# Order of wide and narrow matmuls in two accumulations of an attention, expert and MLP kernel

## The chip, the cores and the metric

The kernel runs on one core of a Trainium2 chip. The metric is the device time of one execution in microseconds. Before the change it is 5529.54 us, the median of 3 runs (5529.25 to 5530.24).

## The reference

Three layers follow one another, in float32:

```python
# attention: u, v (8, 3072, 256), z (8, 3072, 64)
scores = (1.0 / S) * np.matmul(z, z.transpose(0, 2, 1))
attn = np.maximum(scores, 0.0) ** 2
x = (u * np.matmul(attn, v)).reshape(B * S, D)          # 24576 rows of 256
# experts: 8 of them, each row goes to one
xn, en = x / (norm(x) + 1e-6), emb / (norm(emb) + 1e-6)
logits = xn @ en.T / tau
expert_idx = argmax(logits); gate_w = softmax(logits)[expert_idx]
out[mask_e] = gate_w * (np.maximum(x[mask_e] @ w1[e], 0) @ w2[e])   # w1 256x1024, w2 1024x256
# MLP: w_in 256x2048, w_out 2048x256
h = x @ w_in
g = np.where(h > 0, h, np.exp(np.minimum(h, 0)) - 1)
return g @ w_out
```

## The kernel before, in words

TensorE works on float32r operands. To keep float32's accuracy, an operand is split into `hi`, its float32r part, and `lo`, the rest, and a product is made of three: hi x hi, hi x lo and lo x hi. In the two accumulations that the change touches the right-hand tile holds both parts side by side: columns 0 to 255 are the hi part of v (or of w_out), columns 256 to 511 its lo part. One matmul with `hi` as weights over all 512 columns gives hi x hi and hi x lo at once, and one with `lo` as weights over the first 256 columns gives lo x hi, added onto the first half.

The work is a list of steps, which a loop at L1328 emits in order. In step n the loop emits the first matmuls of step n (`"h"`), the splitting of step n-1 on VectorE (`"d1"` to `"d4"`), any matmuls due here such as transposes (`pre`), the accumulation of step n-2 (`"acc"`, since LAG is 2), the elementwise part of step n on ScalarE (`"g"`), and then the loads, stores and small operations that were planned for the step. Each engine runs its instructions in this order.

Attention has 48 chunks of 512 query rows and 12 steps for each, 576 in all. `att_h` (L358) makes four 512-column matmuls for 256 keys, ScalarE takes relu and square, ScalarE or VectorE makes `hi`, VectorE `lo`, and `att_acc` (L401) adds `hi`, `lo` times v onto four accumulators, one for each 128 query rows `q`, for the two key tiles `j`. The last step of a chunk empties accumulators 0 and 1 as soon as they are done, then 2 and 3.

After that come units of the expert stage and of the MLP, mixed: 41 A units (512 rows of one expert, four steps with 512-column matmuls), 21 B units (256 rows, two steps with 256-column matmuls), 41 M units (the MLP of an A unit) and 7 D units (the MLP of rows that B units made). M and D have eight steps each. In one, `m_h` (L926) makes twelve 512-column matmuls, ScalarE and VectorE work out the activation and split it, and `m_acc` (L1019) is the same accumulation as in attention, with w_out in place of v. The very last D unit has functions of its own (`l_h`, `l_acc`). `xt_ops` (L835) transposes the rows of an A or D unit, eight small matmuls that stand ahead of the accumulation two steps before that unit starts.

`hi` and `lo` take slots of one ring of 48; a slot is free when its last reader is done. Every matmul is emitted by the helper at L102, so that all have this line in the profile, and each has a weight load of its own (its first operand).

Of the kernel before, what the change touches and what calls it, by code (L numbers as in the profile page):

```python
# [27 lines left out]
def attn_moe_mlp(ctx, tc, zT, u, v, emb, tau, wp, w_in, w_out, out):  # L28
# [99 lines left out]
    loadD, loadA = defaultdict(float), defaultdict(float)  # L128

    def fill(L, n0, n1, d, a, off):  # L130
        """steps for L operations, in order, that even out the load of their engine"""
        load, c, o = (loadD, d, off) if d else (loadA, a, 0)
        n1 = max(n1, n0 + 1)
        if not c:
            return [n0 + i * (n1 - n0) // L for i in range(L)]
        lo, hi = 0.0, 100.0
        for _ in range(40):
            mid = (lo + hi) / 2
            fits = sum(int(max(0.0, mid - load[w + o]) / c + 0.5) for w in range(n0, n1))
            lo, hi = (lo, mid) if fits >= L else (mid, hi)  # L140
        out = []
        for w in range(n0, n1):
            out += [w] * int(max(0.0, hi - load[w + o]) / c + 0.5)
        out = out[:L]
        for w in out:
            loadD[w + off] += d
            loadA[w] += a
        return out
# [4 lines left out]
            tasks[w][s].append(fn)  # L153

    def pairs(fns, n0, n1, d=0.0, a=0.0):
        """the second half of each pair comes a step after the first"""
        s = stream()
        for i, w in enumerate(fill(len(fns) // 2, n0, n1, d, a, 1)):
            tasks[w][s].append(fns[2 * i])
            tasks[w + 1][-s].append(fns[2 * i + 1])  # L160
# [68 lines left out]
                         zt.bitcast(F32).rearrange("p (t d) -> p t d", t=4))  # L229

    def inv_norm_ops(n2, inv, w):
        """inv = 1/(sqrt(n2)+1e-6) as a list of single operations"""
        h = {}

        def a0():
            h["z"] = t_sm()[:, :w]
            h["t"] = t_sm()[:, :w]
            ts(h["t"].bitcast(I32), n2.bitcast(I32), 1, ALU.logical_shift_right)
        ops = [a0, lambda: ts(h["z"].bitcast(I32), h["t"].bitcast(I32), -1, ALU.mult, 0x5F3759DF, ALU.add)]
        for c in (1.0, 0.25, 0.0625):  # L240
            ops += [lambda c=c: stt(h["t"], h["z"], c, n2, ALU.mult, ALU.mult),
                    lambda: tt(h["t"], h["t"], h["z"], ALU.mult),
                    lambda: stt(h["z"], h["t"], 3.0, h["z"], ALU.subtract, ALU.mult)]
        ops += [lambda: stt(h["t"], h["z"], -0.125, n2, ALU.mult, ALU.mult),
                lambda: ts(h["t"], h["t"], 1e-6, ALU.add),
                lambda: vec.reciprocal(inv, h["t"])]
        return ops
# [27 lines left out]
            return fn  # L275
        return [ld], [n2(e) for e in range(E)] + [late] + [sc(e) for e in range(E)]

# [1 line left out]
    P, Q, V, X, XE, UT, AC, HL, PS = {}, {}, {}, {}, {}, {}, {}, {}, {}  # L279
    n2t, dott = {}, {}  # L280

    def z_ops(b, c2, parts=1):
        """P = [hi; lo], Q = [lo; hi] of two chunks"""
        h = {}

        def ld(w=slice(0, 2)):
            if "z" not in h:
                h["z"] = slot("zz")
            src = zT[b, :, c2 * 1024 + w.start * 512:c2 * 1024 + w.stop * 512]
            for q in range(2):  # L290
                sp.dma_start(flat(h["z"][:, w])[q * 64:(q + 1) * 64], src)

        def o1(w):
            def fn():
                if (b, c2) not in P:
                    P[b, c2] = rslot("zp")
                cp(P[b, c2][:, w], h["z"][:, w])
            return fn

        def o2(w):  # L300
            def fn():
                p = P[b, c2][64:128, w]
                tt(p, h["z"][64:128, w], f(p), ALU.subtract)
            return fn
        def direct(w):
            def fn():
                for d, nm in ((P, "zp"), (Q, "zq")):
                    if (b, c2) not in d:
                        d[b, c2] = rslot(nm)
                z_, p, q = h["z"][:, w], P[b, c2][:, w], Q[b, c2][:, w]  # L310
                cp(p[0:64], z_[0:64])
                cp(q[64:128], z_[64:128])
                tt(q[0:64], z_[0:64], f(p[0:64]), ALU.subtract)
                tt(p[64:128], z_[64:128], f(q[64:128]), ALU.subtract)
            return fn
        ws = [slice(i * 2 // parts, (i + 1) * 2 // parts) for i in range(parts)]
        if c2 == 0 == b:
            return ld, [direct(w) for w in ws]
        return ld, [o for w in ws for o in (o1(w), o2(w))]
# [81 lines left out]
    def att_acc(C, m):  # L401
        b, c = divmod(C, NC)
        if m == 0:
            AC[C] = [t_acc(), t_acc()]
        hi, lo = HL.pop((C, m))
        last = m == CS - 1
        vt = V[b, m]
        for q in range(4):
            a = AC[C][q // 2][:, q % 2]
            sl = slice(q * 128, q * 128 + 128)  # L410
            for j in range(2):
                st = last and j == 1
                mm(a, hi[:, j, sl], vt[:, j], m == 0 and j == 0, st)
                mm(a[:, :256], lo[:, j, sl], vt[:, j, :256], False, st)
            if last and q % 2 == 1:
                if q == 1:
                    X[C] = slot("x", F32, (4, 256))
                    XE[C] = slot("xe", F32, (4, 256))
                ap = AC[C][q // 2]
                cp(XE[C][:, q - 1:q + 1], ap[:, :, 256:])  # L420
                cp(X[C][:, q - 1:q + 1], ap[:, :, :256])
# [157 lines left out]
            return fn  # L579
        return seg1, rank, seg2, [scat(t) for t in range(T)], [scale(t) for t in range(T)]  # L580

# [1 line left out]
    arena = {}  # L583

    def keep(name, shape, dt=F32):
# [75 lines left out]
        tt(o[:, :, 1:], c[:, :, :E - 1], c[:, :, 1:], ALU.subtract)  # L661

    def tile_plan_ops(J, Fn, cumF, tag, taken):
        """first rows of J full tiles and their experts' weight rows"""
        h = {}

        def k3(n):
            h[n] = keep(n + tag, [128, J, E])
            return h[n]

        def k2(n):
            h[n] = keep(n + tag, [128, J])
            return h[n]

        ops = [
            lambda: tt(k3("cmp"), b2(K["jt"][:, :J], J, E), bj(K[cumF], J), ALU.is_ge),
            lambda: red(k2("e"), h["cmp"], ALU.add),
            lambda: ts(k2("w"), h["e"], 128.0, ALU.mult, K["pcol"], ALU.add),
            lambda: vec.tensor_copy(keep("wi" + tag, [128, J], I32), h["w"]),
            lambda: ts(keep("reg" + tag, [128, E]), K[Fn], -512.0, ALU.mult, float(N), ALU.add),  # L680
            lambda: tt(k3("t"), h["cmp"], bj(K["reg" + tag], J), ALU.mult),
            lambda: red(k2("s"), h["t"], ALU.add),
            lambda: stt(h["s"], K["jt"][:, :J], 512.0, h["s"], ALU.mult, ALU.add),
            lambda: onehot(k3("oh"), h["cmp"]),
        ]
        if taken is None:
            ops += [lambda: red(keep("taken" + tag, [128, E]), h["oh"].rearrange("p j e -> p e j"), ALU.add)]
        else:
            ops += [
                lambda: tt(h["oh"], h["oh"], bj(K[taken], J), ALU.mult),  # L690
                lambda: red(k2("ta"), h["oh"], ALU.add),
                lambda: stt(h["s"], h["ta"], 512.0, h["s"], ALU.mult, ALU.add)]

        def ix():
            h["ix"] = keep("ixf" + tag, [128, J, 4])
            tt(h["ix"], b2(h["s"], J, 4), tpj(J, 4), ALU.add)
        return ops + [ix, lambda: vec.tensor_copy(keep("ix" + tag, [128, J, 4], I32), h["ix"])]
# [68 lines left out]

        return ops + [arena.clear]

# [1 line left out]
    W1, W2, XT, IDS, WST, WI, WO, X2 = {}, {}, {}, {}, {}, {}, {}, {}  # L770

    def gather(dst, src, idx, bound):
# [60 lines left out]
        return [gi(t) for t in range(nt)] + [gx(t) for t in range(nt)], h  # L833

    def xt_ops(key, h, dst, nt):  # L835
        """transposes of the rows and their two parts"""
        def tr():
            p = t_ps()
            h["p"] = p if nt == 4 else p[:, 0].rearrange("p (a b) -> p a b", a=2)
# [179 lines left out]
    def m_acc(key, i):  # L1019
        if i == 0:  # L1020
            AC[key] = [t_acc(), t_acc()]
        hi, lo = HL.pop((key, i))
        w = WO[i]
        last = i == NF2 // 2 - 1
        for q in range(4):
            a = AC[key][q // 2][:, q % 2]
            sl = slice(q * 128, q * 128 + 128)
            for j in range(2):
                st = last and j == 1
                mm(a, hi[:, j, sl], w[:, j], i == 0 and j == 0, st)  # L1030
                mm(a[:, :256], lo[:, j, sl], w[:, j, :256], False, st)
            if last and q % 2 == 1:
                if q == 1:
                    PS[key] = slot("o", F32, (4, 256)), slot("o2", F32, (4, 256))
                o, t = PS[key]
# [25 lines left out]
        return ld, xt_ops(key, h, X2, 4)  # L1061

    def conv_ops(src, store):
        """float64 weights, as their words, into two float32r parts"""
        h = {}

        def ld():
# [63 lines left out]
            return fn  # L1131
        return [li(fq, kc) for fq in range(FF // 512) for kc in range(2)] + [lo(g) for g in range(NF2 // 2)]

# [1 line left out]
    groups = []  # L1135
    for b in range(B):
        c0 = b * NC
# [42 lines left out]
        for i in range(nst[un[0]]):  # L1180
            steps.append((lf if un == units[-1] else fns[un[0]], (un, i)))

    # attention inputs
    for n in range(T0):
        loadA[n] += 2.0
        loadD[n + 1] += 1.2
# [81 lines left out]
    p2 = max(w + 7, start["A", NA1] - 18)  # L1268
    spread(plan2_ops(), w + 1, p2, 0.35)

    # MLP weights
    cb = conv_blocks()
    for i, (ld, ops) in enumerate(cb):
        L = (NCH - 4) * CS // len(cb)
# [103 lines left out]
```

## Time and profile before

| | before |
|---|---|
| time, median of 3 runs | 5529.54 us |
| span of the profiled execution (from its first to its last instruction; the profile has no other time of it) | 5525.6 us |
| TensorE matmuls, busy | 5500.0 us, 28836 instructions |
| TensorE weight loads, busy | 4673.7 us |
| VectorE busy | 4239.6 us |
| ScalarE busy | 4101.0 us |
| GpSimd busy | 1402.7 us |
| granted TensorE clock, mean | 0.999 |

In the rows PE is TensorE's matmuls, PEld its weight loads, DVE VectorE, ACT ScalarE. `psa<-v,hi` means: writes the accumulator tile psa, reads v and hi; `pss` are the tiles of the first matmuls of a step, `zp` and `zq` the two parts of z, `wo` w_out's tile, `xh`, `xl`, `x2h`, `x2l` the split rows of the expert stage and the MLP, `w` the experts' weights. A row of the timeline gives the start in us, the length in us, and how many like instructions in a row are merged into it (x24). Matmul records overlap, so the time that one takes up on the engine is read from its start to the start of the next.

### The profile page before, as it was taken

To read this page: it belongs to the slowest core of one execution; us is meant where nothing else is said; L and a number is where in the kernel's file an instruction comes from. 1 tells how busy PE (TensorE), PEld (TensorE's weight loads), DVE (VectorE), ACT (ScalarE), POOL (GpSimd) and SP (SyncE) were. 2 spreads that over 40 slices of the span, in tenths; PEclk is the share of its full clock that TensorE was granted. 3 is DMA by queue.
4 is the path that set the end of the run, shared out by engine and by line. 5 is a ranking of instruction groups with operands and counts; after the bars stand their busy time and mean duration, and the time that the engine had idled before them with its cause. 6 is when DMAs were issued, how large, how long until landed. Compare 5 with 4: busy or idle time off the path is not lost. (4 is left out here: it accounts for less than half of the span.)

```text
span 5525.6 us, 77428 instructions
## 1 busy us (share of the span) xinstructions
PE 5500.0 (100%) x28836; PEld 4673.7 (85%) x28836; DVE 4239.6 (77%) x7911; ACT 4101.0 (74%) x4882; POOL 1402.7 (25%) x1207
## 2 busy tenths in 40 slices
PE   9999999999999999999999999999999999999998
PEld 7888888888888888888888888888888888888887
DVE  7888888888788878887776677667767676777887
ACT  7888888888888887666666666666666666666776
POOL 0010101011111113323443444344434122221011
PEclk9999999999999999999999999999999999999999
DMA  3222112222212212312221222122212111110000
GB/s 94 62 58 58 51 57 54 54 54 54 62 50 65 50 35 81 88 50 67 67 82 63 81 64 82 65 82 65 81 62 78 33 50 53 52 48 27 20 24 20
DMA packets 176360, 324.05 MB, mean 59 GB/s; under 512 B 34348, under 2 KB 117807, under 8 KB 175984
## 3 DMA queue, kind: packets, MB, share of 16 engines
q0 software_dynamic: 76896, 206.62, 12.2%
q1 hardware_dynamic: 99088, 112.49, 7.3%
q8 instruction: 228, 3.74, 0.3%
q14 instruction: 148, 1.21, 0.1%
HBM read 241.55 MB, written 67.23 MB: 56 GB/s over the span
## 5 line engine op out<-in xcount | busy, mean ns | idle before, releaser
L102 PE MATMUL psa<-v,hi 128*128 128x512 f32 x4608 | 1649.5, 398 | 0.6 <-DVE hi L389 0.6
L102 PE MATMUL psa<-v,lo 128*128 128x256 f32 x4608 | 1295.2, 281 | 1.5 <-DVE lo L81 1.5
L102 PE MATMUL psa<-wo,hi 128*128 128x512 f32 x3072 | 1099.1, 398 | 0.6 <-DVE hi L1010 0.6
L102 PEld LDWEIGHTS psa<-v,hi 128*128 128x128 f32 x4608 | 866.5, 188 | 211.3 <-DVE hi L389 1.4
L102 PEld LDWEIGHTS psa<-v,lo 128*128 128x128 f32 x4608 | 871.9, 189 | 28.0 <-DVE lo L81 2.1
L81 DVE TENSOR_TENSOR lo<-r,hi 128x1024 fp32r<-128x1024 f32 x576 | 705.3, 1225 | 217.7 <-ACT hi L99 208.1
L102 PE MATMUL psa<-wo,lo 128*128 128x256 f32 x3072 | 861.1, 280 | 0.9 <-DVE lo L81 0.8
L102 PE MATMUL pss<-x2h,wi 128*128 128x512 f32 x2624 | 817.0, 392 | 0.8 <-ACT r L927 0.8
L91 DVE SCALAR_TENSOR_TENSOR y<-e,y 128x1024 f32<-128x1024 f32 x384 | 469.9, 1224 | 395.9 <-ACT e L995 392.0
L368 ACT ACTIVATE r<-pss 128x1024 f32<-128x1024 f32 x576 | 590.7, 1026 | 237.2 <-PE pss L102 223.8
L942 ACT ACTIVATE e<-pss 128x1024 f32<-128x1024 f32 x376 | 386.3, 1027 | 441.4 <-PE pss L102 437.3
L102 PEld LDWEIGHTS psa<-wo,hi 128*128 128x128 f32 x3072 | 576.9, 188 | 136.4 <-DVE hi L1010 1.0
L373 ACT ACTIVATE r<-r 128x1024 f32<-128x1024 f32 x576 | 611.8, 1062 | 17.1
L778 POOL DMA_INDIRECT out<-o,ids x192 | 207.7, 1082 | 1563.0 <-ACT hi L869 564.6
L93 DVE SCALAR_TENSOR_TENSOR junk<-x,en 128x256 f32<-128x256 f32 x1536 | 601.4, 420 | 0.1
L102 PEld LDWEIGHTS psa<-wo,lo 128*128 128x128 f32 x3072 | 579.3, 189 | 14.3 <-DVE lo L81 1.5
L869 ACT ACTIVATE hi<-pss 128x1024 fp32r<-128x1024 f32 x206 | 211.7, 1028 | 501.1 <-PE pss L102 501.1
L567 POOL DMA_INDIRECT tok<-idt,pi x192 | 229.4, 1195 | 1378.3 <-DVE pi L546 751.0
L102 PEld LDWEIGHTS pss<-x2h,wi 128*128 128x128 f32 x2624 | 475.3, 188 | 98.6 <-ACT r L927 1.1
L102 PE MATMUL pss<-x2l,wi 128*128 128x512 f32 x1312 | 513.9, 392 | 0.0
L81 DVE TENSOR_TENSOR y<-r,y 128x1024 f32<-128x1024 f32 x384 | 470.8, 1226 | 33.9 <-DVE y L91 1.4
L81 DVE TENSOR_TENSOR lo<-y,hi 128x1024 fp32r<-128x1024 f32 x384 | 470.6, 1226 | 17.7
(168 smaller groups left out, 10116.1 us busy)
## 6 DMA issues: line engine op xcount, KB each, us to landing
vs<-v SPq DMA_DIRECT2D x48, 512.0 KB, 5.0
u<-u SPq DMA_DIRECT2D x48, 512.0 KB, 4.0
xs<-x SPq DMA_DIRECT2D x48, 512.0 KB, 4.5
zz<-zT SPq DMA_DIRECT2D x46, 256.0 KB, 4.6
zq<-zp POOLq DMA_DIRECT2D x46, 256.0 KB, 3.6
w<-w_in SPq DMA_DIRECT2D x8, 512.0 KB, 4.1
wis<-hl SPq DMA_DIRECT2D x8, 512.0 KB, 2.9
w<-w_out SPq DMA_DIRECT2D x8, 512.0 KB, 4.3
```

Source lines behind the costliest of these rows:

```text
L81: vec.tensor_tensor(out=o, in0=a, in1=b, op=op)
L91: vec.scalar_tensor_tensor(out=o, in0=a, scalar=s, in1=b, op0=op0, op1=op1)
L93: vec.scalar_tensor_tensor(out=o, in0=a, scalar=s, in1=b, op0=op0, op1=op1, accum_out=acc)
L102: pe.matmul(o, lhsT=l, rhs=r, start=start, stop=stop, skip_group_check=True)
L368: act.activation(out=r, in_=p, func=AF.Relu, scale=1.0 / S)
L373: act.activation(out=r, in_=r, func=AF.Square)
L567: pool.indirect_dma_start(out=tok[:, :], out_offset=bass.IndirectOffsetOnAxis(ap=h["pi"][:, t:t + 1], axis=0), in_=K["idt"][:, gt:gt + 1], ...
L778: pool.indirect_dma_start(out=dst, out_offset=bass.IndirectOffsetOnAxis(ap=idx, axis=0), in_=src, in_offset=None, bounds_check=bound, oob_ ...
L869: act.activation(out=hi, in_=p, func=AF.Relu)
L942: act.activation(out=e, in_=p, func=AF.Relu, scale=-1.0)
```

## The change

In `att_acc` and in `m_acc` the sixteen matmuls of a step are put in another order. Before, for each accumulator `q` and each half `j`, the 512-column one with `hi` is followed by the 256-column one with `lo`. After, all eight with `hi` come first (in the same order of `q` and `j`), then all eight with `lo`. In the last step of a chunk or unit this is done for accumulators 0 and 1 first and then for 2 and 3, with the copies behind each half, as before.

```diff
-        for q in range(4):
-            a = AC[C][q // 2][:, q % 2]
-            sl = slice(q * 128, q * 128 + 128)
-            for j in range(2):
-                st = last and j == 1
-                mm(a, hi[:, j, sl], vt[:, j], m == 0 and j == 0, st)
-                mm(a[:, :256], lo[:, j, sl], vt[:, j, :256], False, st)
-            if last and q % 2 == 1:
+        for qs in ((0, 1), (2, 3)) if last else ((0, 1, 2, 3),):
+            for part in range(2):
+                for q in qs:
+                    a = AC[C][q // 2][:, q % 2]
+                    sl = slice(q * 128, q * 128 + 128)
+                    for j in range(2):
+                        st = last and j == 1
+                        if part == 0:
+                            mm(a, hi[:, j, sl], vt[:, j], m == 0 and j == 0, st)
+                        else:
+                            mm(a[:, :256], lo[:, j, sl], vt[:, j, :256], False, st)
+            if last:
+                q = qs[1]
                 if q == 1:
                     X[C] = slot("x", F32, (4, 256))
...
```

The hunk in `m_acc` is the same with `w = WO[i]` in place of `vt`. Some comments are dropped besides.

## Rows read from the trace of the kernel before

**Rows 1.** The page, busy time of each engine: share of span, instructions.
```profile
PE 5500.0 (100%) x28836; PEld 4673.7 (85%) x28836; DVE 4239.6 (77%) x7911; ACT 4101.0 (74%) x4882; POOL 1402.7 (25%) x1207
```
**Rows 2.** Groups of instructions: busy us, mean ns of one | idle before.
```profile
L102 PE MATMUL psa<-v,hi 128*128 128x512 f32 x4608 | 1649.5, 398 | 0.6 <-DVE hi L389 0.6
...
L102 PE MATMUL psa<-wo,hi 128*128 128x512 f32 x3072 | 1099.1, 398 | 0.6 <-DVE hi L1010 0.6
...
L102 PEld LDWEIGHTS psa<-v,lo 128*128 128x128 f32 x4608 | 871.9, 189 | 28.0 <-DVE lo L81 2.1
```
**Rows 3.** Waits of TensorE: us in total, times, longest.
```profile
PE pss L102 <- DVE zp L81: 5.7, 1, 5.7
PE psa L102 <- DVE lo L81: 2.3, 3, 0.8
```
**Rows 4.** Timeline of TensorE in attention; columns in the first line.
```profile
start us, us, engine line op out<-in xcount [idle before <-releaser]
...
2000.12 0.39 PE L102 MATMUL psa<-v,hi 128*128 128x512 f32 x1
2000.35 0.28 PE L102 MATMUL psa<-v,lo 128*128 128x256 f32 x1
2000.46 0.40 PE L102 MATMUL psa<-v,hi 128*128 128x512 f32 x1
...
2000.82 0.40 PE L102 MATMUL psa<-v,hi 128*128 128x512 f32 x1
2001.06 0.28 PE L102 MATMUL psa<-v,lo 128*128 128x256 f32 x1
2001.18 0.40 PE L102 MATMUL psa<-v,hi 128*128 128x512 f32 x1
...
2037.72 0.39 PE L102 MATMUL psa<-v,hi 128*128 128x512 f32 x1
```
**Rows 5.** Timeline of TensorE in an M unit: four starts.
```profile
3658.32 0.39 PE L102 MATMUL psa<-wo,hi 128*128 128x512 f32 x1
...
3661.13 0.64 PE L102 MATMUL pss<-x2h,wi 128*128 128x512 f32 x2
...
3663.92 0.39 PE L102 MATMUL psa<-wo,hi 128*128 128x512 f32 x1
...
3675.10 0.39 PE L102 MATMUL psa<-wo,hi 128*128 128x512 f32 x1
```
**Rows 6.** Timeline of TensorE in the expert stage, A and B units.
```profile
2598.67 0.61 PE L102 MATMUL pss<-xh,w 128*128 128x512 f32 x2
...
2601.39 0.61 PE L102 MATMUL psa<-hi,w 128*128 128x512 f32 x2
...
2604.11 3.04 PE L102 MATMUL pss<-xb,w 128*128 128x256 f32 x24
2606.98 0.63 PE L102 MATMUL psa<-hi,w 128*128 128x512 f32 x2
...
2609.73 3.04 PE L102 MATMUL pss<-xb,w 128*128 128x256 f32 x24
```
**Rows 7.** Timeline of TensorE around transposes ahead of an MLP block.
```profile
3680.70 0.79 PE L842 MATMUL pss<-ident,rows 128*128 128x128 f32 x8
3681.33 0.46 PE L102 MATMUL psa<-wo,hi 128*128 128x512 f32 x1
...
3684.18 0.62 PE L102 MATMUL pss<-x2h,wi 128*128 128x512 f32 x2
...
3686.92 0.39 PE L102 MATMUL psa<-wo,hi 128*128 128x512 f32 x1
```
**Rows 8.** Busy us of each engine in a window of attention: PE, PEld, DVE, ACT, POOL.
```profile
1000.00:1500.00 500.00, 500.00 (x2667) 425.17 (x2666) 413.74 (x1224) 435.99 (x530) 65.46 (x58) 1.00 0.22 56
```

## The prediction before the run

> **What bounds the kernel now.** I read the shares of busy time first: TensorE's matmul row is busy 5500.0 us of the 5525.6 us span [rows 1]. That alone only says matmuls never leave a visible gap, because their records overlap: a 512-column matmul is recorded with 398 ns [rows 2], yet the next one starts sooner than that. So the second view is the list of waits of TensorE: the longest entry is the 5.7 us at the very start, and all waits for a late `lo` add up to 2.3 us [rows 3]. Nothing else in the kernel holds TensorE up, so the time is the sum of the intervals from one matmul's start to the next one's, and the third view, the timeline, has to give those. Every term below is a difference of start times there.
>
> In attention one step is four score matmuls and the sixteen of the accumulation. Ten steps run from 2000.12 to 2037.72, 3.760 us each [rows 4]. In turns, a 512-column matmul keeps TensorE for about 0.235 us (0.23 at 2000.12, 0.24 at 2000.82) and a 256-column one for about 0.12 (2001.06 to 2001.18) [rows 4]. In the MLP three steps run from 3658.32 to 3675.10, 5.593 us each: 2.81 for the sixteen in turns and 2.79 for the twelve 512-column matmuls of the next first layer [rows 5].
>
> The rows that matter for the change are those of the expert stage, where the two sizes already run in blocks. Twelve 512-column matmuls in a settled stream take 2598.67 to 2601.39, 2.72 us or 0.2267 each. Twenty-four 256-column ones in a row take 2604.11 to 2606.98, 2.87 us or 0.1196 each. The twelve 512-column ones right after them take 2606.98 to 2609.73, 2.75 us, 0.03 over the settled stream [rows 6]. So one 512 and one 256, each in its block, cost 0.346 us, where a pair in turns costs 2.81 / 8 = 0.351; and the twelve 512s that follow cost 2.75 after a block of 256s but 2.79 after turns. A change of size seems to unsettle the spacing of the 512s that come next, and turns change size sixteen times per block.
>
> **The change part by part.** No instruction is added or removed: the same sixteen matmuls with the same operands, each with its own weight load, in another order. No DMA, and no instruction of another engine, is moved in its queue.
>
> *Attention step, 528 of the 576 (48 chunks, eleven of twelve steps).* The new order gives twelve 512s in a row (four scores, eight `hi`), behind eight 256s. Twelve 512s behind 256s: 2.75. Eight 256s: 2.87 less sixteen at 0.12, 0.95 [rows 6]. Sum 3.70 against 3.760: 0.060 less, times 528 is 31.7 us.
>
> *MLP step, 281 of 376.* (41 M and 7 D units have eight steps; the last unit has its own function and stays, so 47 x 8 = 376 blocks.) Twelve 512s behind 256s 2.75, eight more settled 8 x 0.2267 = 1.81, eight 256s 0.95: 5.51 against 5.593, 0.083 less, times 281 is 23.3 us.
>
> *Last steps, 48 and 47.* They keep two halves, so that the first two accumulators can be emptied early: one more change of size to and fro. I charge it the 0.03 that a start behind 256s costs: gains of 0.03 and 0.053, together 1.4 + 2.5 = 3.9 us. Each half still ends after the same eight matmuls, so the copies of ScalarE start no later.
>
> *MLP blocks behind transposes, 48.* Eight small transposes stand ahead of one block per A and D unit; that block takes 2.85 and the twelve 512s behind it 2.74 [rows 7], the latter already as low as after 256s. With the first `hi` still slow behind the transposes I give these nothing.
>
> *Waits.* `lo`, the last product of the chain, is now wanted by the ninth matmul instead of the second, 7 x 0.2267 = 1.6 us later. The 2.3 us of waits for it [rows 3] contain one of 0.8 in the last unit, which stays; 1.5 goes. `hi` is wanted at the same moment as before, behind the same four or twelve matmuls. Its slot comes free earlier and that of `lo` at the same place.
>
> *Other engines.* Steps get 1.6% shorter, so the same work of ScalarE, 436 us in 500, becomes 443, and VectorE's 414 becomes 420 [rows 8]. Both stay under 90%, the products have two steps of lead, and TensorE waits for neither today. I take nothing for it; were that cover gone, the gain would stop where the engine reached 100%, which at 1.6% it can't.
>
> Sum: 31.7 + 23.3 + 3.9 + 1.5 = 60.4 us. The profile gives for its execution the span alone, 5525.6; the median of the runs is 5529.54, 3.9 above it, for what lies around the span. I carry the difference over: 5529.5 - 60.4 = 5469.
>
> **Bounds.** What the trace doesn't show is eight 256s in a block between 512s (it has 24), with `hi` and `lo` as weights. For the 512s the low end is the settled 0.2267 throughout: 0.03 less in each of 952 steps, 29 us more gain. The high end is the 2.79 that twelve take after turns [rows 5]: attention then gains 0.02 and the MLP 0.043 a step. For the 256s the low end is 0.11, what the first one behind a 512 takes (2000.35 to 2000.46) [rows 4]: eight at 0.88, 0.07 under my 0.95. The high end is that each takes its recorded weight load, 189 ns [rows 2]: 1.51. I take 0.1196, the nearest row, because it holds over 24 in a row with a weight load each, and 2.75, because it stands directly behind such a block.
>
> **The rivals.**
>
> *The order is worth nothing.* If a matmul kept TensorE for a time set by its columns alone, the sum over the same sixteen would be the same: 5529.5. For it speaks that the pair differs by only 0.005 us, half the resolution of one start. Against it, 0.2267 is a mean over twelve settled matmuls and 0.235 one over whole blocks in turns, and twelve behind turns take 2.79 where twelve settled take 2.72 [rows 5, 6]. [...] Chance 0.05.
>
> *Half of it.* Eight 256s are too few to settle, and the 512s behind them go as behind turns: 576 x 0.02 + 281 x 0.04 is 23 us, with 1.5 for the waits and a little for the last steps some 26: 5503. For it: the run of 24 is three times as long. Against: a single 256 in turns already shows 0.11 to 0.12. Chance 0.08.
>
> *Slower: the weight loads come into the open.* In turns every second load lies beside a 512-column matmul, in the new order seven loads in a row lie beside 256-column ones. A load is recorded with 189 ns [rows 2]; if a run of `lo` loads went at that pace, a block of 256s would take 1.51 instead of 0.95, 0.56 more in each of 952 steps: 533 us, so 5469 + 533 = 6002. It decides from 0.1196 + 60 / (952 x 8) = 0.127 us per 256 upward. Against it stand the 24 loads at 0.1196 [rows 6]; for it, that those weights came from other tiles, long ready. Chance 0.03.
>
> **How the numbers follow.** Forecast 0.84, with its own range 5455 to 5483: a sixth of a step's gain either way, and a few us of new waits of an engine that is 1.6% fuller. The low end of the bounds taken whole (5440 by the 512s) I hold for unlikely, since 2.75 is a row. To leave out no more than 2 in 10 I reach towards the half: 5453 to 5500. About 0.2%, 11 us, is what a measurement of this kernel tells from no change. Faster by more: the forecast and the half, 0.92; same 0.05; slower 0.03.
>
> **What would show it.** In the timeline after, an attention step of 3.70 us and an inner MLP step of 5.51; eight `lo` matmuls from first start to the next 512's in 0.95; twelve 512s behind them in 2.75; a TensorE wait list without `lo` of attention. A step of 3.76 shows the first rival, 512s at 2.79 behind a block the second, `lo` matmuls over 0.127 apart the third. The prediction is wrong if steps shorten as said and the span doesn't: then a wait for ScalarE or VectorE has come in, and the list of waits names it.

## The result, and the profile after

The changed kernel takes 5470.52 us (median of 4 runs, 5468.34 to 5471.47) against 5529.65: a ratio of 0.9892 (95% interval 0.9878 to 0.9906), 59 us less. A second measurement, beside experiments 9 and 10, gave 5469.72 and 0.9894 (0.9878 to 0.9911). The spans of the two profiled executions, 5525.6 and 5466.6 us, differ by 59.0 as well.

The page's first part, to hold beside [rows 1]:

```profile
PE 5442.1 (100%) x28836; PEld 4679.9 (86%) x28836; DVE 4238.7 (78%) x7911; ACT 4099.8 (75%) x4882; POOL 1400.4 (26%) x1207
```

The counts are the same on every engine, the work of the other engines is the same within 3 us, and TensorE is as full as before. The same 28836 matmuls simply follow each other more closely. The timeline of TensorE in attention, to hold beside [rows 4] (start, length, form, how many merged):

```profile
2000.12 1.98 PE L102 MATMUL psa<-v,hi 128*128 128x512 f32 x8
2001.94 1.11 PE L102 MATMUL psa<-v,lo 128*128 128x256 f32 x8
2002.89 0.40 PE L102 MATMUL pss<-zp 128*128 128x512 f32 x1
...
2003.82 1.98 PE L102 MATMUL psa<-v,hi 128*128 128x512 f32 x8
2005.64 1.11 PE L102 MATMUL psa<-v,lo 128*128 128x256 f32 x8
...
2010.29 0.40 PE L102 MATMUL pss<-zp 128*128 128x512 f32 x1
...
2014.01 0.40 PE L102 MATMUL pss<-zp 128*128 128x512 f32 x1
```

From 2000.12 to 2003.82 is a step of 3.70 us, before 3.760. The eight `lo` take 2001.94 to 2002.89, 0.95; the eight `hi` take 1.82, 0.2275 each; the four scores behind the `lo`, the first to feel the change back to 512 columns, take 0.93, 0.2325 each. The twelve 512s behind the `lo` take 2002.89 to 2005.64, 2.75. From 2010.29 to 2014.01 stands the last step of a chunk, with its two halves: 3.72. The first expert matmul behind attention, in the trace before and in the one after, shows what attention gained as a whole, 36.1 us:

```profile
2188.11 0.64 PE L102 MATMUL pss<-xh,w 128*128 128x512 f32 x2
```

```profile
2151.99 0.63 PE L102 MATMUL pss<-xh,w 128*128 128x512 f32 x2
```

The MLP, beside [rows 5] and [rows 7]:

```profile
3619.33 1.98 PE L102 MATMUL psa<-wo,hi 128*128 128x512 f32 x8
3621.14 1.11 PE L102 MATMUL psa<-wo,lo 128*128 128x256 f32 x8
3622.10 0.63 PE L102 MATMUL pss<-x2h,wi 128*128 128x512 f32 x2
...
3624.84 1.98 PE L102 MATMUL psa<-wo,hi 128*128 128x512 f32 x8
...
3636.51 2.08 PE L102 MATMUL psa<-wo,hi 128*128 128x512 f32 x8
3638.43 1.11 PE L102 MATMUL psa<-wo,lo 128*128 128x256 f32 x8
3639.38 0.63 PE L102 MATMUL pss<-x2h,wi 128*128 128x512 f32 x2
```

An inner step runs from 3619.33 to 3624.84, 5.51 us, before 5.593; its twelve 512s behind the `lo` take 2.74. The block behind eight transposes takes 3636.51 to 3639.38, 2.87, where such a block took 2.85 before: nothing gained there. The list of waits of TensorE, beside [rows 3] (us in total, times, longest):

```profile
PE pss L102 <- DVE zp L81: 5.7, 1, 5.7
PE pss L102 <- ACT r L932: 1.1, 2, 1.0
PE psa L102 <- DVE lo L81: 0.8, 1, 0.8
```

What is left of the waits for `lo` is the one of the last unit. The wait for `r`, ScalarE's part of an MLP step, stood in the list before too, with 0.8 us.

### The profile page after: what moved, and what is told of

Read it like the earlier page. It is cut to its first block, busy times and chain, and to the rows that moved or that the text cites. A ratio compares the mean times of both kernels' runs of the same rounds, so it can differ in the third digit from the quotient of the medians.

```text
span 5466.6 us, 77438 instructions
## 1 busy us (share of the span) xinstructions
PE 5442.1 (100%) x28836; PEld 4679.9 (86%) x28836; DVE 4238.7 (78%) x7911; ACT 4099.8 (75%) x4882; POOL 1400.4 (26%) x1207
## 3 DMA queue, kind: packets, MB, share of 16 engines
q8 instruction: 228, 3.74, 0.3%
## 4 chain that ended last, share of the span: by engine, by line
PE 99%; DMA 0%; ACT 0%; issue 0%; DVE 0%; POOL 0%; SPq 0%; POOLq 0%; ACTq 0%; DVEq 0%
PE psa L102 59%; PE pss L102 39%; PE pss L847 1%; DMA wst<-wp,wia 0%; DMA out<-o,ids 0%; DMA zz<-zT 0%; ACT y L999 0%; POOL out L783 0%; DVE junk L93 0%; ACT e L947 0%; ACT r L932 0%; POOLq L1383 0%; SPq L291 0%; DVE lo L91 0%; ACT e L1000 0%
## 5 line engine op out<-in xcount | busy, mean ns | idle before, releaser
L102 PE MATMUL psa<-v,hi 128*128 128x512 f32 x4608 | 1152.7, 390 | 0.6 <-DVE hi L389 0.6
L102 PE MATMUL psa<-wo,hi 128*128 128x512 f32 x3072 | 779.7, 391 | 0.8 <-DVE hi L1015 0.6
L102 PEld LDWEIGHTS psa<-v,lo 128*128 128x128 f32 x4608 | 635.0, 190 | 49.0
L102 PE MATMUL psa<-v,lo 128*128 128x256 f32 x4608 | 649.8, 282 | 0.0
L102 PE MATMUL pss<-zp 128*128 128x512 f32 x1152 | 453.7, 394 | 5.9 <-DVE zp L81 5.7
L102 PEld LDWEIGHTS psa<-wo,lo 128*128 128x128 f32 x3072 | 428.6, 190 | 35.2 <-DVE lo L81 1.5
```

What stands on the lines that cost most here:

```text
L102: pe.matmul(o, lhsT=l, rhs=r, start=start, stop=stop, skip_group_check=True)
```

## The experiments

The theory, called S in the expectations: a change of the number of columns from one matmul to the next unsettles the spacing of those that follow, and the order in turns makes sixteen such changes in a step. Its rivals: the turning between the `hi` and `lo` tiles (T), two neighbours of unlike size on one accumulator (P), and waits.

**1 and 2. The order in one place only.** Each is the changed kernel with the other function as before:

```diff
 # 1: att_acc as after; m_acc:            # 2: m_acc as after; att_acc:
-        for qs in ((0, 1), (2, 3)) if last else ((0, 1, 2, 3),):
+        for q in range(4):
...
```

> The new order in attention x v alone, the MLP as before. Theory (S): a change of the column count unsettles the spacing of the 512-column matmuls that follow, so each attention step shortens by itself: 3.70 us instead of 3.76 in 528 steps, 3.73 in 48, no wait for lo: 34 us less than before, 5495 to 5497. Rival: the gain came from elsewhere (other engines meeting other waits): the two halves don't add up to the whole 59 us.

> The new order in the second MLP matmul alone, attention as before. Theory (S): an inner MLP step takes 5.51 us instead of 5.593, 26 us less than before, 5503 to 5505; with the attention-only version 59 to 60 us together. Rival: the halves don't add up.

Attention alone: 5492.47 us, ratio 0.9935 (0.9918 to 0.9951), 3 us under its forecast. MLP alone: 5503.5, ratio 0.9953 (0.9936 to 0.9970). In spans, one profiled execution each, the two gain 5525.6 - 5489.6 = 36.0 and 5525.6 - 5502.3 = 23.3, together 59.3 of the 59.0. By the medians, against the 5528.71 of the kernel before in the same set of runs, they gain 36.2 and 25.2, together 61.4 of 59.1. Within some 2 us the halves add up. Closer than that they can't be read: the one wait for `r` alone is 2.5 us in the list of 2 and absent from that of 1.

**3. Sizes in turns, one tile.** From the kernel before; the product lo x hi is left out:

```diff
-                mm(a[:, :256], lo[:, j, sl], vt[:, j, :256], False, st)
+                mm(a[:, :256], hi[:, j, sl], vt[:, j, :256], False, st)
```

> The order of before (512 and 256 in turns), but the 256-column matmuls take hi as weights too, so that lo is never read: sizes in turns, one tensor; the product lo x hi is left out. Theory (S): the sizes in turns cost the same as before, 3.76 us an attention step and 5.59 an MLP step, 5528 to 5530. Rival (T): turning between two weight tiles (or waiting for lo) was the cost: 3.70 and 5.51, about 5470. Rival (P, 512 and 256 columns in turns into one accumulator): as S.

Measured 5526.27 us, ratio 0.9996 (0.9986 to 1.0006): no change. In its timeline the sixteen, merged into one row that gives the form of the first, and the score matmuls around them:

```profile
2003.23 0.40 PE L102 MATMUL pss<-zp 128*128 128x512 f32 x1
...
2004.18 2.98 PE L102 MATMUL psa<-v,hi 128*128 128x512 f32 x16
2006.99 0.40 PE L102 MATMUL pss<-zp 128*128 128x512 f32 x1
```

From 2003.23 to 2006.99 is 3.76 us. One tile serves all sixteen and no `lo` is waited for, and the cost stays. T and the waits fall.

**4. Sizes in turns, neighbours on unlike accumulators.** The `lo` matmuls of row block q stand beside the `hi` of block q + 1:

```diff
+        for q in range(5):
+            for j in range(2):
+                if q < 4:
+                    one(q, 0, j)        # hi, 512 columns
+                if q:
+                    one(q - 1, 1, j)    # lo, 256 columns
```

> Sizes still in turns for six of eight pairs, but each 256-column matmul goes to the accumulator of the row block before, so that two neighbours never write the same one; all products kept. Theory (S): six pairs in turns at 0.353 and two each at the ends: 3.745 us an attention step, about 5.56 an MLP step, 5505 to 5515. Rival (P): the cost was two neighbours of unlike size on one accumulator: 3.70 and 5.51, about 5470.

Measured 5501.03 us, ratio 0.9948 (0.9928 to 0.9968), a little under the forecast of S and far from P's 5470. In its timeline:

```profile
2003.87 0.52 PE L102 MATMUL psa<-v,lo 128*128 128x256 f32 x3
...
2005.15 0.85 PE L102 MATMUL psa<-v,hi 128*128 128x512 f32 x3
2005.85 0.28 PE L102 MATMUL psa<-v,lo 128*128 128x256 f32 x1
...
2007.61 0.52 PE L102 MATMUL psa<-v,lo 128*128 128x256 f32 x3
```

A step is 3.74 us. The turns begin behind three `hi` and end in three `lo`, so five pairs stand in turns, not six; that is the difference to my 3.745. P falls.

**5. Tiles in turns, one size.** From the kernel before; `lo` over all 512 columns, so a fourth product is added:

```diff
-                mm(a[:, :256], lo[:, j, sl], vt[:, j, :256], False, st)
+                mm(a, lo[:, j, sl], vt[:, j], False, st)
```

> The order of before, hi and lo in turns on the same accumulator, but the lo matmuls run over all 512 columns too: tensors in turns, one size, more work (a fourth product is added). Theory (S): without a change of size all 512s are settled at 0.2267 us: an attention step of 20 takes 4.53 us, an MLP step of 28 takes 6.35, about 6258 in all. Rival (T): turning between the tiles unsettles them, 0.235 each in the block: 4.71 and 6.55, about 6440.

Measured 6258.21 us in one run, as S had it. In its timeline two starts of the same matmul of a step:

```profile
2001.95 0.39 PE L102 MATMUL psa<-v,hi 128*128 128x512 f32 x1
...
2006.49 0.39 PE L102 MATMUL psa<-v,hi 128*128 128x512 f32 x1
```

Twenty 512-column matmuls take 4.54 us, 0.227 each, the settled spacing of [rows 6], although the tiles turn and each pair shares an accumulator. Experiments 3 and 5 together leave the change of size as the cause. What in it costs the time they don't say: every matmul in these runs has a weight load of its own, and whether the loads have a part in it isn't tested.

**6, 7, 11 and 12. How many changes of size, and in runs of what length.** The changed kernel with the groups of row blocks altered:

```diff
-        for qs in ((0, 1), (2, 3)) if last else ((0, 1, 2, 3),):
+        for qs in ((0,), (1,), (2,), (3,)):                               # 6, 11: two hi, two lo
+        for qs in ((0, 1), (2, 3)):                                       # 7: four and four
+        for qs in ((0, 1), (2, 3)) if last else ((0,), (1, 2, 3)):        # 12: two, then six
```

> Each accumulator's two hi matmuls, then its two lo: four changes of size to and fro in a step instead of eight (before) or one (after). Theory (S): each cycle costs what the first matmuls behind a change show (512s 0.233 and 0.236, 256s 0.113 and 0.119): 0.701 for four, 3.73 us an attention step, 5.55 an MLP step, 5497 to 5502. Were it the first of each kind alone that is late, or the number of changes alone, the same within 5 us; were only the last change avoided of use, 5525.

> In every step what the change does in the last one: four hi, four lo, four hi, four lo. Two cycles a step. Theory (S): 3.72 us an attention step and 5.53 an MLP step, as the last steps of the changed kernel take: 5482 to 5488.

Groups of two: 5464.6 us, far under my 5497 to 5502 and no slower than the changed kernel. Groups of four: 5493.36, over my 5482 to 5488. Both miss, on opposite sides, so a fixed cost for each cycle of wide and narrow is wrong. The timeline of the groups of four:

```profile
2000.53 1.09 PE L102 MATMUL psa<-v,hi 128*128 128x512 f32 x4
2001.46 0.63 PE L102 MATMUL psa<-v,lo 128*128 128x256 f32 x4
2001.93 1.09 PE L102 MATMUL psa<-v,hi 128*128 128x512 f32 x4
2002.86 0.64 PE L102 MATMUL psa<-v,lo 128*128 128x256 f32 x4
...
2004.27 1.07 PE L102 MATMUL psa<-v,hi 128*128 128x512 f32 x4
...
2007.98 1.09 PE L102 MATMUL psa<-v,hi 128*128 128x512 f32 x4
```

Steps of 3.74 and 3.71: these 512s don't settle, four `hi` take 0.93 where settled ones take 0.907. The two lengths take turns almost all through attention (3.734 and 3.713 in the trace), though the order of sizes is the same in every step. So the sizes of the nearest neighbours alone don't fix the spacing. I ran the groups of two again and split the case: one short run of `lo` between long runs of `hi`.

> Groups of two again, with more rounds: four changes to and fro a step, yet 5464.6 us where theory S with a fixed cost per cycle had 5497 to 5502. If that stands, 5463 to 5467, below the changed kernel's 5468 to 5472, with attention steps of 3.69 us; if it was chance, 5470 or above.

> Two hi, two lo, six hi, six lo in every step but the last of a chunk or unit: one short run of two lo between long runs of hi, and one long run of lo. If each change back to 512 columns costs the whole 0.0275 us whatever the length of the run before it: 3.72 us an attention step, 5.53 an MLP step, about 5488. If a run of two lo leaves most of it out: only the first two 512s behind it are late, 3.70 to 3.71, 5470 to 5478. If groups of two are cheap only because each is followed by another before the spacing settles, 5488.

Groups of two again: 5462.46 us, ratio 0.9876 (0.9860 to 0.9893). Two then six: 5486.39, ratio 0.9921 (0.9902 to 0.9941). First the timeline of the groups of two, then that of two and six:

```profile
2000.37 0.61 PE L102 MATMUL psa<-v,hi 128*128 128x512 f32 x2
2000.82 0.40 PE L102 MATMUL psa<-v,lo 128*128 128x256 f32 x2
2001.06 0.63 PE L102 MATMUL psa<-v,hi 128*128 128x512 f32 x2
2001.53 0.39 PE L102 MATMUL psa<-v,lo 128*128 128x256 f32 x2
2001.75 0.63 PE L102 MATMUL psa<-v,hi 128*128 128x512 f32 x2
...
2003.15 0.40 PE L102 MATMUL pss<-zp 128*128 128x512 f32 x1
...
2004.06 0.62 PE L102 MATMUL psa<-v,hi 128*128 128x512 f32 x2
```

```profile
2002.57 0.62 PE L102 MATMUL psa<-v,hi 128*128 128x512 f32 x2
2003.03 0.40 PE L102 MATMUL psa<-v,lo 128*128 128x256 f32 x2
2003.26 1.55 PE L102 MATMUL psa<-v,hi 128*128 128x512 f32 x6
2004.65 0.88 PE L102 MATMUL psa<-v,lo 128*128 128x256 f32 x6
...
2006.29 0.62 PE L102 MATMUL psa<-v,hi 128*128 128x512 f32 x2
```

In two and six, the six `hi` behind only two `lo` take 2003.26 to 2004.65, 1.39 where settled ones take 1.36: a run of two unsettles as much as a long one, the whole 0.03, and the step is 3.72. In groups of two the four scores behind the last `lo` take 0.91 (2003.15 to 2004.06), close to settled, where they take 0.93 in the changed kernel. Single pairs are too short for starts given to 0.01 us, so here are averages over the ordinary steps of attention in each trace, in us, against settled ones (twelve 512s at 0.2267 and eight 256s at 0.120, together 3.680):

| order | changes of size in a step | 512s lose | 256s gain | step |
|---|---|---|---|---|
| turns (before) | 16 | 0.103 | 0.023 | 3.760 |
| groups of two | 8 | 0.052 | 0.038 | 3.693 |
| groups of four | 4 | 0.057 | 0.014 | 3.723 |
| two and six | 4 | 0.054 | 0.015 | 3.719 |
| the change | 2 | 0.029 | 0.008 | 3.702 |

The first two 256s behind a change come sooner than settled ones (0.113 and 0.119 in the changed kernel), the 512s behind one come later. In groups of two every 256 is one of the first two behind a change, and that gives back most of what the 512s lose, while the 512s lose no more than with half as many changes. So the cost isn't a price per change but depends on where the next change falls. Two matmuls apart the two sides nearly cancel, one or four apart they don't. Why the spacing moves at all, these traces can't tell.

**8, 9 and 10. Fewer changes than the change itself has.** `lo` of two (9) or four (10) steps is kept and multiplied together behind the `hi` of the last of them; 8 is the changed kernel beside them.

```diff
+        LO[C].append((lo, vt))
+        los = LO.pop(C) if m % 2 == 1 else []      # 10: m % 4 == 3
...
+            for n_, (lo_, r_) in enumerate(los):
...
+                        mm(a[:, :256], lo_[:, j, sl], r_[:, j, :256], False, ...)
```

> The changed kernel again, beside the two that follow: 5468 to 5472.

> lo of an even step is kept and multiplied right behind lo of the next odd step: runs of 16 of 256 columns and of 24 (attention) or 40 (MLP) of 512, half as many changes of size as in the changed kernel. Theory (S): a cycle costs 0.0275 us in the 512s behind it less 0.008 in the first two 256s, so 0.010 us less a step: attention 3.690 a step, MLP 5.504, 8 to 9 us less than the changed kernel, 5461 to 5463. Rival: the gain of the change came from the waits for lo or from its place late in the step, and no more is to be had: 5470; or slots of the ring held a step longer make VectorE or ScalarE wait: slower than the changed kernel.

> The same with lo of four steps together: a quarter of the changes of size. Theory (S): 0.0145 us less a step than the changed kernel, some 12 to 13 us: 5457 to 5460, unless the three more slots of the ring that it holds make an engine wait, which would show in its waits. Rival: as before, 5470 or slower.

Measured 5469.72, 5465.22 (ratio 0.9882, 0.9865 to 0.9898) and 5469.07 (0.9896, 0.9879 to 0.9912). By the medians half of the forecast gain came in 9, none in 10, though the intervals of all three overlap. Yet undisturbed steps are as forecast. The starts of two neighbouring `lo` runs, two steps apart in 9 and four in 10:

```profile
2015.20 2.08 PE L102 MATMUL psa<-v,lo 128*128 128x256 f32 x16
2022.58 2.08 PE L102 MATMUL psa<-v,lo 128*128 128x256 f32 x16
```

```profile
2025.68 4.00 PE L102 MATMUL psa<-v,lo 128*128 128x256 f32 x32
2040.42 4.00 PE L102 MATMUL psa<-v,lo 128*128 128x256 f32 x32
```

7.38 / 2 = 3.69 and 14.74 / 4 = 3.685 us a step, against 3.70. The rest was given back as waits. The waits of ScalarE for accumulators, first in the changed kernel, then in 10, and behind them one of TensorE in 10:

```profile
ACT o L99 <- PE psa L102: 39.7, 96, 6.6
...
ACT xe L99 <- PE psa L102: 29.3, 88, 0.4
```

```profile
ACT o L99 <- PE psa L102: 174.6, 96, 6.6
...
ACT xe L99 <- PE psa L102: 112.5, 84, 1.8
```

```profile
PE psa L102 <- DVE hi L390: 4.9, 15, 1.0
```

In 10 the last step of a chunk or unit has 32 `lo` matmuls instead of 8, so the accumulators are done later, and the copies out of them stand at the head of ScalarE's queue meanwhile: 287 us of waiting instead of 69. Behind them stand the square and the `hi` of the next steps, and TensorE then waits for `hi`, 15 times. That one follows from the other is read from the order of ScalarE's queue; it fits that 13 of the 18 first `hi` matmuls that start over 0.05 us late in attention stand in the third step of a chunk, whose `hi` is made behind those copies. My rival had named the ring's slots; the waits that grew are those of the copies.

## Why the prediction was right

**What bounds the kernel.** That the time is the sum of the intervals from start to start held: span and steps fell together, and the halves add up within the scatter. The 3.9 us by which the median stood above the span is not what lies around the span, which is 1.7 us in the profiled run after (5468.34 and 5466.6); the rest is likely the difference between one execution and another. The forecast didn't hang on it.

**The size of the terms.** The sum was 60.4, the measured gain 59.1. The steps came as worked out: 3.70, 5.51, eight `lo` in 0.95. But attention was to gain 31.7 + 1.4 + 1.5 for the waits, 34.6, and gained 36.1 in the trace, and the MLP was to gain 25.8, and what follows attention gained 22.9. The two misses have unlike signs, so that the sum came so close is in part luck, though each is hardly larger than the 2 us by which the halves scatter. A last step of attention averages 3.714 where I had charged 3.73. The inner MLP step averages 5.513, a gain of 0.080 and not 0.083, and the blocks behind transposes, put at nothing, take 2.87 where they took 2.85. There are 45 of them and not 48, which is worth 0.2 us.

**Rows of another stage were the right price.** The twelve 512s behind a run of 256s in the expert stage [rows 6] had other tiles, other operands and a run three times as long, and still gave attention and the MLP within 0.01 us a step. Experiments 3 to 5 show why: neither the tile nor the accumulator matters to the spacing, the order of the sizes does.

**Other engines.** The one wait of the matmuls for ScalarE, that for `r`, went from 0.8 to 1.1 us, with steps 1.6% shorter. How near that cover was to its end shows in experiment 10, where the same engines with the same work made TensorE wait once the copies stood longer at the head of ScalarE's queue.

**The rivals.** "Worth nothing" is out. The Trainium skill ("TensorE: Matmul & The Clock Gate", "Back-to-back issue gap") gives columns / 2.4 plus 2.5 ns as the gap of an isolated matmul, 215.8 ns for 512 columns; in the streams of these runs settled 512s take 226.7, and more behind a change of size. Experiments 3 and 5 show that the spacing depends on the neighbours' columns too. "Half of it" is out: twelve 512s take 2.74 to 2.75 behind eight 256s and 2.75 behind 24 [rows 6], and by experiment 12 two unsettle them as much. The weight loads stayed hidden: 0.95 us for eight `lo`, each with its own load.

**Where the reasoning was thin.** "Turns change size sixteen times per block" was right as a description, but the picture behind it, a cost for every change, is not: over a settled step of 12 x 0.2267 + 8 x 0.12 = 3.68, eight changes a step (groups of two) cost some 0.01 us, four (groups of four) 0.04, two (the change) 0.02 and sixteen (turns) 0.08. The prediction didn't need that picture, since it took the changed order's price from rows of the same pattern. Experiments 6 and 7, which leaned on it, missed.

**Which order is best.** The groups of two have the lowest median, 5462.46, below the changed kernel's 5470.52 and 5469.72, with attention steps of 3.693 against 3.702 on average; 0.007 us in each of some 950 steps would be 6.7. All six runs of the groups of two (5459.31 to 5465.53) lie below all eight of the changed kernel (5467.89 to 5472.14), but the two were not measured side by side, and their intervals against the kernel before, 0.9860 to 0.9893 and 0.9878 to 0.9911, overlap. So the groups of two are likely better, which isn't shown.

(`m_h` stands at L930 of the kernel before, not at the line given ahead of the prediction.)

## What to carry to other kernels

Where one engine is full without a visible gap, read its time from start to start, by size and by what stood before; a mean length hides what the neighbours cost. Price a new order by rows in which the same sequence of sizes already runs, even in another stage, and don't turn what you read there into a price per change. And when work is put off to gain spacing, look at what then stands longer at the head of another engine's queue.

## What the runs showed of the hardware that was not expected

- A settled stream of float32r matmuls, each with its own weights, keeps a start every 0.2267 us for 512 columns and 0.120 for 256 at a granted clock of 0.999 (the 2.4 GHz level); over 24 in a row the mean is 0.1196, since the first two come sooner. The 256 columns more cost 0.1067, so by an estimate from these two numbers 0.013 us of either don't hang on the columns.
- Behind a change from 256 to 512 columns the 512s lose about 0.03 us: six take 1.39 instead of 1.36 behind two narrow ones, twelve 2.75 instead of 2.72 behind eight and behind 24.
- Behind a change from 512 to 256 columns the first two 256s come sooner, 0.113 and 0.119 us instead of 0.120. Changes two matmuls apart nearly cancel (3.69 us a step), one or four apart they don't (3.76, 3.72). The cause is open.
